# First-stage weights rounded during attention and kept in DRAM, with the first group's sums parked in DRAM

## The chip, the cores and the metric

The kernel runs on one core of a Trainium2 chip. The metric is the device time of one execution in microseconds (us), the median of several runs. Engines are named as the profile names them: PE (matmul), PEld (its weight load), DVE (VectorE), ACT (ScalarE), POOL (GpSimd) and SP, whose queue issues every DMA here.

## The reference

Three stages follow each other. The first is linear attention over 4 batches of 8 heads, 576 tokens, 64 columns a head; the second an MLP of 2048 hidden columns with a leaky slope per column; the third four dense experts of 1024 hidden columns, weighted by the normalised probabilities.

```
proj = x @ w_phi                               # 64 -> 128, for q and for k
proj = proj - max(abs(proj), axis=-1)
phi  = concat(exp(proj), exp(-proj))           # 256 features
kv, z = k_phi.T @ v, sum(k_phi)
attn = (q_phi @ kv) / (q_phi @ z + 1e-6)
h = attn @ w_in;  g = max(h, 0) + alpha * min(h, 0);  y = g @ w_out        # w_in, w_out come as float64
out = sum_e p[e] * (max(y @ w1[e], 0) @ w2[e])
```

Attention output and `y` are 2304 x 512. The weights of the second stage are float64 in DRAM; the kernel rounds them to float32 itself, with integer operations on the two 32-bit words of each number.

## The kernel before

Every large product runs as three fp32r matmuls: a value is split into a high and a low part, and high x high, high x low and low x high are added in PSUM. The hidden columns of both MLP stages are cut in 48 chunks of 128 (16 of the second stage, then 32 of the experts), four to a group, and the 2304 tokens in blocks of 512, 512, 512, 512 and 256. An up block is 12 matmuls of 512 columns (`up_products`, L208), then the activation (`t`, `gh`, `gl`); a down block is 12 matmuls too (`down_chunk`, L234). The sums of a token block over the groups stay in SBUF, in `acc_a` for the first three blocks and in `acc_b` for the other two.

Attention is worked in 16 pairs of heads. For each pair, keys and queries are projected (L348 to L350, three units of 512, 512 and 256 columns each), DVE takes the largest absolute value (`m`, L355) and subtracts it (`pmk`, `pmq`, L362), ACT takes the exponentials of the keys (`ke`, L368), PE forms `kv` (L379, L385), turns it and the queries, and multiplies them (L437); DVE inverts the denominator (`dt`, `di`, `den`, L449 to L452), POOL multiplies and splits. The order of all this is written by a planner (`Plan.run`): it keeps a time for each engine from estimated costs, and takes at each step the operation that can begin first, by rank where several can. The order is then fixed on each engine, which works in it and waits where something is late. The first weight group is rounded and split in the plan too (operations `W`), and the first group's up and down products for token blocks 0 to 2 are filled in between attention's (`U`, `G0` to `G2`, `M`, `C`).

Rounding one weight tile (128 x 512 numbers) takes a 512 KB read, one ACT scaling (L538 in the plan, L176 after it), four DVE instructions (`words`, L168 to L171), one addition, on DVE or POOL (L542, L178), and the split (two more). In the plan, the staging areas are the unused slots 1 and 2 of `acc_a`, which is why the planner's `C` (the copy of a group's sum into `acc_a`) waits for those areas. The other 24 tiles of the second stage are rounded after the plan by `ahead`/`fetch`/`rounded`, two to five steps before their use, in the main loop.

Of the kernel before, what the change touches and what calls it, by code (L numbers as in the profile page):

```python
# [130 lines left out]
def fused(ctx: ExitStack, tc: tile.TileContext, qT, kT, v_main, v_tail, w_phi, alpha, probs, w64, wcat, out):  # L131
# [22 lines left out]
    acc = [acc_a[:, i] for i in range(NA)]  # L154

    def split(src, hi, lo, hi_eng, lo_eng):
        if hi_eng is nc.scalar:
            nc.scalar.copy(hi, src)  # L158
        else:
            hi_eng.tensor_copy(hi, src)  # L160
        lo_eng.tensor_tensor(lo, src, f32(hi), ALU.subtract)  # L161
# [10 lines left out]

    def rounded(w, r, u):

        lo, hi = w[:, 0::2], w[:, 1::2]
        nc.scalar.mul(f32(r), f32(hi), 2.0**-112)  # L176
        words(r, u, lo, hi)
        nc.vector.tensor_tensor(f32(r), f32(r), f32(u), ALU.add)  # L178

    def fetch(c, half, w, st, u):  # L180

        if c < NF1:
            nc.sync.dma_start(st, w64[c, half])
            rounded(st, w.bitcast(U32), u)
        else:
            nc.sync.dma_start(w, wcat[c - NF1, half])
        raw[c, half] = w
# [90 lines left out]
    with ExitStack() as st1:  # L278
# [8 lines left out]
        for args in (  # L287
            ("kr", 1, F32, P, S), ("qr", 1, F32, P, S), ("v", 1, F32, P, len(TILES), 2, D),
            ("kh", 1, F32R, P, S), ("kl", 1, F32R, P, S), ("qh", 1, F32R, P, S), ("ql", 1, F32R, P, S),
            ("m", 13, F32, P, 4), ("pmk", 2, F32, P, 4, F), ("pmq", 3, F32, P, 4, F), ("ke", 2, F32, P, 4, 2, F),  # L290
            ("kvs", 1, F32, P, 4, F), ("qe", 4, F32, P, 2, HMAX), ("kvt", 4, F32, P, 4, P),
            ("den", 2, F32, P, S), ("dt", 1, F32, P, S), ("num", 2, F32, P, S), ("di", 3, F32, P, S // 32, 1),
            ("gh", 5, F32R, P, BLK), ("gl", 5, F32R, P, BLK), ("t", 2, F32, P, BLK),
        ):
            ring(*args)
# [226 lines left out]


        areas = []
        for i in range(2):
            a = acc[1 + i].bitcast(U32)
            areas.append([a[:, :2 * DM], a[:, 2 * DM:3 * DM], a[:, 3 * DM:4 * DM]])
        plan.bufs["area"] = 2
        early = [(0, 0), (1, 0), (0, 1), (1, 1), (2, 0), (3, 0), (2, 1), (3, 1)]

        def w_step(i, k, e):
            c, half = early[i]
            st64, w, u = areas[i % 2]
            lo, hi = st64[:, 0::2], st64[:, 1::2]
# [16 lines left out]
        for i, (c, half) in enumerate(early):  # L551
            costs = ({"d": 1500}, {"a": act(DM)}, {"v": 2 * dve2(DM) + 2 * dve(DM) + 330}, lo_cost(DM), hi_cost(DM), lo_cost(DM))
            for k, cost in enumerate(costs):
                op(("W", k, c, half), cost, [("W", k - 1, c, half)] * (k > 0), RANK["W"] + WSTEP * i,
                   alloc=[("area", i)] * (k == 0), reads=[("area", i)] * (k == 5), late=2000 * (k == 0),
                   emit=lambda e, i=i, k=k: w_step(i, k, e))
# [16 lines left out]
        for blk in range(NA):  # L573
            tok = sum(BLOCKS[blk])
            have = [("X2", p) for p, (b, j) in enumerate(pairs) if b * S < tok]
            for cs in (tuple(range(GRP)),):
# [12 lines left out]
                for i in range(CC):  # L589
# [43 lines left out]
    def ahead(c, half):  # L633
        w = rpool.tile([P, DM], F32, name="w")
        st = u = None
        if c < NF1:
            st = spool.tile([P, 2 * DM], U32, name="st")
            u = upool.tile([P, DM], U32, name="u")
        fetch(c, half, w, st, u)

# [65 lines left out]
```

## Time and profile before

| | us |
|---|---|
| median of 3 runs (1437.93 to 1438.18) | 1438.12 |
| profiled execution, its own time | 1439.93 |
| its span | 1438.2 |
| PE busy / DVE / ACT / POOL | 1418.9 / 654.7 / 412.4 / 212.4 |

The span is what the profile's times count from and to; the profiled execution took 1.7 us more than it. Busy times are summed over the span, so a share says nothing of one stage. Attention with the first blocks fills about the first 300 us, the second stage goes on to about 630 us, the experts fill the rest.

### The profile page before, as it was taken

How to read it: one execution, taken by the hardware profiler on the slowest of the kernel's cores; microseconds unless marked ns; L12 is line 12 of the kernel's file. 1: busy time of each engine (PE TensorE's matmuls, PEld its weight loads, DVE VectorE, ACT ScalarE, POOL GpSimd, SP SyncE). 2: the span in 40 equal slices, each digit the busy share in tenths (PEclk: the TensorE clock that was granted, in tenths of full speed). 3: DMA queues.
4: the chain of work that ended last, by engine and by line, in shares of the span. 5: the costliest groups of instructions: out<-in, count | busy, mean ns of one | idle time of the engine just before them, and what ended most of it. 6: DMA issues, size and time to landing. Idle time of an engine off the chain costs nothing.

```text
span 1438.2 us, 17632 instructions
## 1 busy us (share of the span) xinstructions
PE 1418.9 (99%) x7200; PEld 1152.1 (80%) x7200; DVE 654.7 (46%) x1067; ACT 412.4 (29%) x857; POOL 212.4 (15%) x165
## 2 busy tenths in 40 slices
PE   7999999999999999999999999999999999999998
PEld 4667667778888888888888888888888888888887
DVE  7966656687958855663222222222222222222222
ACT  6877666632212112232021120121210201211110
POOL 3443223102002002011020020020100200200100
PEclk9999999999999999999999999999999999999999
DMA  4311111130202001001020020010100200100001
GB/s 148 112 50 51 50 50 51 53 103 30 88 1 59 30 8 52 1 23 37 0 59 0 1 59 0 8 52 1 30 30 0 59 0 8 52 0 0 30 30 74
DMA packets 25136, 53.67 MB, mean 37 GB/s; under 512 B 3168, under 2 KB 4320, under 8 KB 25056
## 3 DMA queue, kind: packets, MB, share of 16 engines
q1 hardware_dynamic: 25056, 52.55, 12.2%
q8 instruction: 57, 0.93, 0.3%
q14 instruction: 23, 0.19, 0.0%
HBM read 47.82 MB, written 4.72 MB: 37 GB/s over the span
## 4 chain that ended last, share of the span: by engine, by line
PE 94%; DVE 3%; ACT 1%; DMA 1%; issue 0%; SPq 0%; POOL 0%; ACTq 0%; DVEq 0%; POOLq 0%
PE up L208 39%; PE dn L234 39%; PE bank L437 4%; PE kv L379 3%; PE mm L208 2%; PE kv L385 2%; PE mm L234 2%; PE bank L420 1%; PE bank L348 1%; PE bank L349 1%; PE bank L350 1%; DMA st<-w 1%; DMA acc_a<-w 0%; PE bank L401 0%; DVE m L355 0%
## 5 line engine op out<-in xcount | busy, mean ns | idle before, releaser
L208 PE MATMUL up<-Xl,whu 128*128 128x512 f32 (+1 forms) x912 | 334.6, 367 | 0.0
L208 PE MATMUL up<-Xh,whu 128*128 128x512 f32 (+1 forms) x912 | 334.5, 367 | 0.0
L208 PE MATMUL up<-Xh,wlu 128*128 128x512 f32 (+1 forms) x912 | 334.4, 367 | 0.0
L219 ACT ACTIVATE gh<-up 128x512 fp32r<-128x512 f32 (+1 forms) x160 | 88.7, 555 | 539.5 <-PE up L208 539.4
L220 DVE SCALAR_TENSOR_TENSOR gl<-up,gh 128x512 fp32r<-128x512 f32 (+1 forms) x160 | 102.0, 638 | 303.8 <-ACT gh L219 303.7
L234 PE MATMUL dn<-whd,gh 128*128 128x512 f32 x576 | 224.2, 389 | 0.0
L234 PE MATMUL dn<-wld,gh 128*128 128x512 f32 x576 | 224.2, 389 | 0.0
L234 PE MATMUL dn<-whd,gl 128*128 128x512 f32 x576 | 224.1, 389 | 0.0
L208 PEld LDWEIGHTS up<-Xh,whu 128*128 128x128 f32 x912 | 172.0, 189 | 28.6
L208 PEld LDWEIGHTS up<-Xl,whu 128*128 128x128 f32 x912 | 172.0, 189 | 28.4
L208 PEld LDWEIGHTS up<-Xh,wlu 128*128 128x128 f32 x912 | 171.9, 189 | 28.2
L161 POOL TENSOR_TENSOR wlu<-w,whu 128x512 fp32r<-128x512 f32 x44 | 58.2, 1322 | 915.3 <-ACT whu L158 879.7
L234 PEld LDWEIGHTS dn<-whd,gl 128*128 128x128 f32 x576 | 108.1, 188 | 22.5
L234 PEld LDWEIGHTS dn<-whd,gh 128*128 128x128 f32 x576 | 108.2, 188 | 22.1
L234 PEld LDWEIGHTS dn<-wld,gh 128*128 128x128 f32 x576 | 108.2, 188 | 22.1
L271 DVE SCALAR_TENSOR_TENSOR acc_a<-dn,pr,acc_a 128x512 f32<-128x512 f32 x72 | 50.2, 751 | 135.4 <-PE dn L234 135.4
L234 PE MATMUL dn<-gh,wld 128*128 128x512 f32 (+1 forms) x272 | 99.1, 364 | 0.0
L234 PE MATMUL dn<-gh,whd 128*128 128x512 f32 (+1 forms) x272 | 99.1, 364 | 0.0
L234 PE MATMUL dn<-gl,whd 128*128 128x512 f32 (+1 forms) x272 | 99.0, 364 | 0.0
L158 ACT CAST gh<-t 128x512 fp32r<-128x512 f32 (+1 forms) x68 | 38.6, 569 | 134.8 <-DVE t L224 134.6
L437 PE MATMUL bank<-qe,kvt 128*128 128x256 f32 (+1 forms) x256 | 72.6, 417 | 0.9 <-DVE pmk L362 0.9
L158 ACT CAST whu<-w 128x512 fp32r<-128x512 f32 x44 | 27.3, 620 | 136.4 <-PE up L208 121.4
(121 smaller groups left out, 1734.8 us busy)
## 6 DMA issues: line engine op xcount, KB each, us to landing
w<-wcat SPq DMA_DIRECT2D x64, 256.0 KB, 2.6
st<-w SPq DMA_DIRECT2D x24, 512.0 KB, 3.5
kr<-kT SPq DMA_DIRECT2D x16, 288.0 KB, 2.8
qr<-qT SPq DMA_DIRECT2D x16, 288.0 KB, 2.8
out<-o SPq DMA_DIRECT2D x18, 256.0 KB, 2.0
v<-v_main SPq DMA_DIRECT2D x16, 256.0 KB, 3.0
acc_a<-w SPq DMA_DIRECT2D x8, 512.0 KB, 4.5
v<-v_tail SPq DMA_DIRECT2D x16, 32.0 KB, 2.9
```

What stands on the lines that cost most here:

```text
L158: nc.scalar.copy(hi, src)
L161: lo_eng.tensor_tensor(lo, src, f32(hi), ALU.subtract)
L208: nc.tensor.matmul(ps[:, :bn], a[:, cs], x[:, cc, t0:t0 + bn], start=n == 0, stop=n == 3 * CC - 1)
L219: nc.scalar.activation(gh, ps, AF.Relu)
L220: nc.vector.scalar_tensor_tensor(gl, ps, 0.0, f32(gh), ALU.max, ALU.subtract)
L234: nc.tensor.matmul(ps, a, b, start=start and k == 0, stop=stop and k == 2)
L271: nc.vector.scalar_tensor_tensor(av, ps, pe, av, ALU.mult, ALU.add)
L348: nc.tensor.matmul(o, xh[:, tok], wbh, start=True, stop=False)
L349: nc.tensor.matmul(o, xh[:, tok], wbl, start=False, stop=False)
L379: nc.tensor.matmul(kv[h * D:(h + 1) * D, 0], v[:rows, tile_, h], e[:rows, 2 * i + h], start=tile_ == 0, stop=tile_ == len(TILES) - 1, skip ...
L385: nc.tensor.matmul(kv[r:r + 32, 1], ones[:rows], e[:rows, 2 * i + h], start=False, stop=tile_ + 2 >= len(TILES), tile_position=(0, r), ski ...
L437: nc.tensor.matmul(nd[:, :n], tl["kvt", p][:, 2 * h + s], tl["qe", (p, h, c)][:, s, :n], start=s == 0, stop=s == 1)
```

## The change

All 32 tiles of the second stage's weights are now rounded in the plan. The 24 tiles of groups 1 to 3 are not split there: after the addition they are written to DRAM (`wr`, 256 KB each), and the main loop's `fetch` reads them back as float32, as it reads the experts' weights. All three slots of `acc_a` serve as staging areas until the plan ends. The first group's sums can therefore no longer be kept there: they are copied to a new small tile `co`, written to DRAM (`sums`) and read back into `acc_a` when the plan is through. To make room, `kvt` goes from 4 buffers to 3 and `t` from 2 to 1.

```diff
+    sums = [dram.tile([P, CC * BLK], F32, name=f"sums{i}") for i in range(NA)]
+    wr = {(c, half): dram.tile([P, DM], F32, name=f"wr{c}_{half}") for c in range(GRP, NF1) for half in range(2)}
...
-    def fetch(c, half, w, st, u):
-
-        if c < NF1:
-            nc.sync.dma_start(st, w64[c, half])
-            rounded(st, w.bitcast(U32), u)
-        else:
-            nc.sync.dma_start(w, wcat[c - NF1, half])
+    def fetch(c, half, w):
+
+        nc.sync.dma_start(w, wr[c, half] if c < NF1 else wcat[c - NF1, half])
...
-            ... ("qe", 4, F32, P, 2, HMAX), ("kvt", 4, F32, P, 4, P),
+            ... ("qe", 4, F32, P, 2, HMAX), ("kvt", 3, F32, P, 4, P),
-            ("gh", 5, F32R, P, BLK), ("gl", 5, F32R, P, BLK), ("t", 2, F32, P, BLK),
+            ("gh", 5, F32R, P, BLK), ("gl", 5, F32R, P, BLK), ("t", 1, F32, P, BLK), ("co", 2, F32, P, BLK),
...
-        plan.bufs["area"] = 2
+        plan.bufs["area"] = NA
         early = [(0, 0), (1, 0), (0, 1), (1, 1), (2, 0), (3, 0), (2, 1), (3, 1)]
+        early += [(c + i, half) for c in range(GRP, NF1, GRP) for half in range(2) for i in range(GRP)]
...
+            elif c >= GRP:
+                nc.sync.dma_start(wr[c, half], f32(w))
...
-                    op(("C", *key), copy_cost(BLK), [("M", *key)] + [("W", 5, *x) for x in early[:blk + 6] if blk], ...
-                       ... cp(engines[e], acc[a[1]][:, a[2] * BLK:(a[2] + 1) * BLK], tl["mm", a]))
+                    op(("C", *key), copy_cost(BLK), [("M", *key)], pr_ + RANK["G"] - RANK["U"], alloc=[("co", key)],
+                       reads=[("mm", key)], emit=lambda e, a=key: cp(engines[e], new("co", a), tl["mm", a]))
+                    op(("CD", *key), {"d": 1000}, [("C", *key)], ..., reads=[("co", key)], late=2000,
+                       emit=lambda e, a=key: nc.sync.dma_start(sums[a[1]][:, a[2] * BLK:(a[2] + 1) * BLK], tl["co", a]))
...
             plan.run()
+            for i in range(NA):
+                nc.sync.dma_start(acc[i], sums[i])
```

The order moves most on DVE in attention. Before, DVE comes to the first key unit of the thirteenth pair (pair 12) with nothing but attention behind it; these are the last rows up to that unit's subtraction.

```order
L362 TENSOR_TENSOR pmq<-bank,m 64x256
L325 TENSOR_TENSOR ql<-qr,qh 128x576
L355 TENSOR_REDUCE m<-bank 64x2
L362 TENSOR_TENSOR pmk<-bank,m 64x256
L136 COPY num<-bank 64x320
L449 STREAM_TRANSPOSE dt<-den 128x576
L450 TENSOR_SCALAR di<-dt 128x18
L451 RECIPROCAL di<-di 128x18
L452 STREAM_TRANSPOSE den<-di 128x576
L355 TENSOR_REDUCE m<-bank 128x4 x2
L362 TENSOR_TENSOR pmk<-bank,m 128x512 x2
```

In the changed kernel the same place reads so (L173 to L176 are the four `words` instructions, L349 and L356 the maximum and the subtraction).

```order
L173 TENSOR_SCALAR acc_a<-acc_a 128x512
L174 SCALAR_TENSOR_TENSOR acc_a<-acc_a 128x512
L175 TENSOR_SCALAR acc_a<-acc_a 128x512
L176 SCALAR_TENSOR_TENSOR acc_a<-acc_a 128x512
L564 TENSOR_SCALAR t<-mm,alpha_sb 128x512
L565 SCALAR_TENSOR_TENSOR t<-mm,t 128x512
L173 TENSOR_SCALAR acc_a<-acc_a 128x512
L174 SCALAR_TENSOR_TENSOR acc_a<-acc_a 128x512
L175 TENSOR_SCALAR acc_a<-acc_a 128x512
L176 SCALAR_TENSOR_TENSOR acc_a<-acc_a 128x512
L349 TENSOR_REDUCE m<-bank 128x4 x2
L356 TENSOR_TENSOR pmk<-bank,m 128x512 x2
```

Up to this last row DVE has 31 of the 32 rounding steps behind it now, and had 8 there before; 13 of the first group's 24 blocks stand ahead of it on PE, and 8 did before.

At the end of attention, the first matmul of the main loop (`up`) stood before two more up blocks of the plan (`mm`) on PE:

```order
L208 MATMUL mm<-Xh,wlu 128x512
L208 MATMUL up<-Xh,whu 128x512
L208 MATMUL mm<-Xh,whu 128x512
L208 MATMUL mm<-Xl,whu 128x512
L208 MATMUL mm<-Xh,wlu 128x512
```

In the changed kernel the main loop's first matmuls stand between the down matmuls of the plan's last chunk (L202 is the up product, L228 the down product):

```order
L228 MATMUL mm<-gl,whd 128x512
L202 MATMUL up<-Xh,whu 128x512
L202 MATMUL up<-Xl,whu 128x512
L202 MATMUL up<-Xh,wlu 128x512
L202 MATMUL up<-Xh,whu 128x512
L202 MATMUL up<-Xl,whu 128x512
L202 MATMUL up<-Xh,wlu 128x512
L228 MATMUL mm<-gh,whd 128x512
L228 MATMUL mm<-gh,wld 128x512
L202 MATMUL up<-Xh,whu 128x512
L228 MATMUL mm<-gl,whd 128x512
```

Twelve blocks of the first group (four down, four up, four down) came after attention's last product on PE before; seven (three up, four down) come after it now.

On SP's queue, which carried only loads of `kr`, `qr` and `v` in this stage once the eight early reads were through, writes that wait for their data now stand ahead of loads:

```order
L540 DMA wr_1_96<-acc_a 128x512
L540 DMA wr_1_98<-acc_a 128x512
L532 DMA acc_a<-w 128x1024
L599 DMA sums_80<-co 128x512
L540 DMA wr_0_99<-acc_a 128x512
L532 DMA acc_a<-w 128x1024 x2
L331 DMA kr<-kT 128x576
L331 DMA qr<-qT 128x576
```

Each read of a weight tile (L532) waits until the write out of its area has landed, and the next pair's loads wait behind both.

## Rows read from the trace of the kernel before

**Rows 1.** The page's first part: busy time, share of the span, instructions.
```profile
PE 1418.9 (99%) x7200; PEld 1152.1 (80%) x7200; DVE 654.7 (46%) x1067; ACT 412.4 (29%) x857; POOL 212.4 (15%) x165
```

**Rows 2.** Busy time by stretch: length, each engine (instructions), clock, DMA share, GB/s.
```profile
0.00:35.00 35.00, 26.28 (x175) 17.01 (x175) 25.62 (x44) 22.19 (x50) 12.68 (x18) 0.95 0.46 142
35.00:70.00 35.00, 32.70 (x221) 21.74 (x221) 33.89 (x54) 29.29 (x72) 17.73 (x13) 1.00 0.39 124
105.00:280.00 175.00, 175.00 (x1152) 123.19 (x1151) 103.06 (x192) 119.35 (x293) 51.01 (x37) 1.00 0.17 49
280.00:315.00 35.00, 32.34 (x138) 25.46 (x137) 33.40 (x59) 15.70 (x29) 4.56 (x3) 1.00 0.31 91
```

**Rows 3.** DVE's groups by form, 0 to 300 us: busy us, mean ns, idle before.
```profile
L355 DVE TENSOR_REDUCE m<-bank 128x4 f32<-128x512 f32 x64 | 41.5, 674 | 2.5 <-PE bank L350 2.3
...
L362 DVE TENSOR_TENSOR pmk<-bank,m 128x512 f32<-128x512 f32 x32 | 20.6, 675 | 0.0
L355 DVE TENSOR_REDUCE m<-bank 64x2 f32<-64x256 f32 x32 | 13.1, 409 | 8.6 <-PE bank L350 8.6
L452 DVE STREAM_TRANSPOSE den<-di 128x576 f32<-128x576 f32 x16 | 12.4, 778 | 0.6
L449 DVE STREAM_TRANSPOSE dt<-den 128x576 f32<-128x576 f32 x16 | 12.4, 777 | 41.2 <-ACT den L136 41.2
L170 DVE TENSOR_SCALAR acc_a<-acc_a 128x512 uint32<-128x512 uint32 x8 | 8.5, 1065 | 0.6
...
L564 DVE TENSOR_SCALAR t<-mm,alpha_sb 128x512 f32<-128x512 f32 x9 | 6.7, 747 | 6.8 <-PE mm L208 6.8
...
L171 DVE SCALAR_TENSOR_TENSOR acc_a<-acc_a 128x512 f32<-128x512 uint32 x8 | 6.5, 812 | 0.3
L565 DVE SCALAR_TENSOR_TENSOR t<-mm,t 128x512 f32<-128x512 f32 x9 | 6.2, 691 | 0.3
L169 DVE SCALAR_TENSOR_TENSOR acc_a<-acc_a 128x512 uint32<-128x512 uint32 x8 | 5.5, 692 | 0.3
L168 DVE TENSOR_SCALAR acc_a<-acc_a 128x512 uint32<-128x512 uint32 x8 | 4.4, 547 | 2.2 <-ACT acc_a L538 2.2
L451 DVE RECIPROCAL di<-di 128x18 f32<-128x18 f32 x16 | 4.3, 267 | 0.5
...
L450 DVE TENSOR_SCALAR di<-dt 128x18 f32<-128x18 f32 x16 | 3.4, 213 | 0.5
```

**Rows 4.** Timeline, DVE and POOL: start, us, engine, line, operation, operands.
```profile
44.27 0.40 DVE L168 TENSOR_SCALAR acc_a<-acc_a 128x512 uint32<-128x512 uint32 x1
44.70 0.69 DVE L169 SCALAR_TENSOR_TENSOR acc_a<-acc_a 128x512 uint32<-128x512 uint32 x1
...
45.02 1.66 POOL L325 TENSOR_TENSOR ql<-qr,qh 128x576 fp32r<-128x576 f32 x1 [2.03 <-ACT qh L136]
...
45.50 1.46 DVE L170 TENSOR_SCALAR acc_a<-acc_a 128x512 uint32<-128x512 uint32 x1
```

**Rows 5.** Timeline at a key unit of pairs 4 and 12: ACT, DVE, PE.
```profile
76.11 1.15 ACT L368 ACTIVATE ke<-pmk 128x512 f32<-128x512 f32 x2
...
77.58 0.41 DVE L362 TENSOR_TENSOR pmk<-bank,m 64x256 f32<-64x256 f32 x1
...
212.63 1.08 PE L379 MATMUL kv<-ke,v 128*64 128x256 f32 x8
```

**Rows 6.** Timeline of PE after attention: two neighbours, and the two waits.
```profile
293.10 0.39 PE L234 MATMUL mm<-gl,whd 128*128 128x512 f32 x1
293.33 0.39 PE L208 MATMUL mm<-Xh,whu 128*128 128x512 f32 x1
...
300.70 0.50 PE L208 MATMUL mm<-Xh,whu 128*128 128x512 f32 x1 [1.72 <-DVE t L565]
...
304.89 0.50 PE L208 MATMUL mm<-Xh,whu 128*128 128x512 f32 x1 [0.94 <-DVE t L565]
```

**Rows 7.** The page's sixth part: DMA issues, KB each, median us to landing.
```profile
acc_a<-w SPq DMA_DIRECT2D x8, 512.0 KB, 4.5
```

More of the change, by code (lines that the diff above doesn't have):

```diff
@@ L136, in cp @@
         (eng.copy if eng is nc.scalar else eng.tensor_copy)(o, i)
+    dram = pool("dram", 1, space=bass.MemoryType.DRAM)
     const = pool("const", 1)
@@ L171, in words @@
         nc.vector.scalar_tensor_tensor(f32(u), lo, 2.0**-52, f32(u), ALU.mult, ALU.mult)
[L173 to L178, printed above, removed]
-    def fetch(c, half, w, st, u):
-        if c < NF1:
-            nc.sync.dma_start(st, w64[c, half])
-            rounded(st, w.bitcast(U32), u)
-        else:
-            nc.sync.dma_start(w, wcat[c - NF1, half])
+    def fetch(c, half, w):
+        nc.sync.dma_start(w, wr[c, half] if c < NF1 else wcat[c - NF1, half])
         raw[c, half] = w
@@ L290, in fused @@
             ("m", 13, F32, P, 4), ("pmk", 2, F32, P, 4, F), ("pmq", 3, F32, P, 4, F), ("ke", 2, F32, P, 4, 2, F),
-            ("kvs", 1, F32, P, 4, F), ("qe", 4, F32, P, 2, HMAX), ("kvt", 4, F32, P, 4, P),
+            ("kvs", 1, F32, P, 4, F), ("qe", 4, F32, P, 2, HMAX), ("kvt", 3, F32, P, 4, P),
             ("den", 2, F32, P, S), ("dt", 1, F32, P, S), ("num", 2, F32, P, S), ("di", 3, F32, P, S // 32, 1),
-            ("gh", 5, F32R, P, BLK), ("gl", 5, F32R, P, BLK), ("t", 2, F32, P, BLK),
+            ("gh", 5, F32R, P, BLK), ("gl", 5, F32R, P, BLK), ("t", 1, F32, P, BLK), ("co", 2, F32, P, BLK),
         ):
@@ L524, in fused @@
         areas = []
-        for i in range(2):
-            a = acc[1 + i].bitcast(U32)
+        for i in range(NA):
+            a = acc[i].bitcast(U32)
             areas.append([a[:, :2 * DM], a[:, 2 * DM:3 * DM], a[:, 3 * DM:4 * DM]])
-        plan.bufs["area"] = 2
+        plan.bufs["area"] = NA
         early = [(0, 0), (1, 0), (0, 1), (1, 1), (2, 0), (3, 0), (2, 1), (3, 1)]
+        early += [(c + i, half) for c in range(GRP, NF1, GRP) for half in range(2) for i in range(GRP)]
         def w_step(i, k, e):
             c, half = early[i]
-            st64, w, u = areas[i % 2]
+            st64, w, u = areas[i % NA]
             lo, hi = st64[:, 0::2], st64[:, 1::2]
@@ L551, in fused @@
         for i, (c, half) in enumerate(early):
-            costs = ({"d": 1500}, {"a": act(DM)}, {"v": 2 * dve2(DM) + 2 * dve(DM) + 330}, lo_cost(DM), hi_cost(DM), lo_cost(DM))
+            costs = [{"d": 1500}, {"a": act(DM)}, {"v": 2 * dve2(DM) + 2 * dve(DM) + 330}, lo_cost(DM)]
+            costs += [hi_cost(DM), lo_cost(DM)] if c < GRP else [{"d": 1000}]
+            end = len(costs) - 1
             for k, cost in enumerate(costs):
                 op(("W", k, c, half), cost, [("W", k - 1, c, half)] * (k > 0), RANK["W"] + WSTEP * i,
-                   alloc=[("area", i)] * (k == 0), reads=[("area", i)] * (k == 5), late=2000 * (k == 0),
+                   alloc=[("area", i)] * (k == 0), reads=[("area", i)] * (k == end), late=2000 * (k == 0 or end == k == 4),
                    emit=lambda e, i=i, k=k: w_step(i, k, e))
@@ L595, in fused @@
                        emit=lambda e, a=key: down_products(a[0], a[1], a[2], new("mm", a)))
-                    op(("C", *key), copy_cost(BLK), [("M", *key)] + [("W", 5, *x) for x in early[:blk + 6] if blk], pr_ + RANK["G"] - RANK["U"],
-                       reads=[("mm", key)], emit=lambda e, a=key: cp(engines[e], acc[a[1]][:, a[2] * BLK:(a[2] + 1) * BLK], tl["mm", a]))
+                    op(("C", *key), copy_cost(BLK), [("M", *key)], pr_ + RANK["G"] - RANK["U"], alloc=[("co", key)],
+                       reads=[("mm", key)], emit=lambda e, a=key: cp(engines[e], new("co", a), tl["mm", a]))
+                    op(("CD", *key), {"d": 1000}, [("C", *key)], pr_ + RANK["G"] - RANK["U"], reads=[("co", key)], late=2000,
+                       emit=lambda e, a=key: nc.sync.dma_start(sums[a[1]][:, a[2] * BLK:(a[2] + 1) * BLK], tl["co", a]))
         with tc.manual_schedule():
@@ L612, in fused @@
             plan.run()
+            for i in range(NA):
+                nc.sync.dma_start(acc[i], sums[i])
             nc.sync.dma_start(pr, probs)
@@ L621, in fused @@
     wb = [pool("wu2", 2), pool("wd2", 1)]
-    spool = pool("stage", 2)
     rpool = pool("raw", 5)
-    upool = pool("u", 1)
     opool = pool("o", 3)
@@ L634, in ahead @@
         w = rpool.tile([P, DM], F32, name="w")
[L635 to L639, printed above, removed]
+        fetch(c, half, w)
     steps = [(grp, blk) for grp in range(NG) for blk in range(NB)][NA:]
```

## The prediction

> **What bounds the kernel now.** I read the page's first part: PE is busy 99% of the span [rows 1], so nothing done beside PE pays, and time can only be won or lost where PE waits. The stretches show where that is [rows 2]: between 105 and 280 us PE is busy all the time; it is short of full only in the first 70 us (26.28 of 35, then 32.70 of 35) and around the end of attention (32.34 of 35). In the second stretch DVE is busy 33.89 of 35 us: there DVE sets the pace, and it carries the eight early rounding steps. From 105 to 280 us DVE is busy 103.06 of 175 us. At the end of attention DVE is full again (33.40 of 35), with weights being rounded, and PE waits for it twice, 1.72 and 0.94 us [rows 6]. The granted clock is 1.00, the 2.4 GHz level, in all of these but the first stretch (0.95) [rows 2].
>
> So before, the 24 late rounding steps cost PE at most these two waits, 2.7 us together. That is all the change can win there; what it can lose is in attention.
>
> **What goes.** The late rounding leaves DVE, and those two waits were for DVE's `t`. In the changed order three up blocks follow attention. A block takes 12 matmuls of 0.233 us, 2.80 us (293.10 to 293.33) [rows 6]. Counting from the end of attention's last product, DVE first has the last pair's division (2.04 us, from about 0.9 us on) and then the three activations, each 1.44 us for `t` [rows 3] and, taken like one of its two instructions, 0.7 each for `gh` and `gl`, one after the other since `t` has one buffer: `gl` is there at 5.7, 9.3 and 12.1 us. PE is through with the up blocks at 8.4, with nine down matmuls at 10.5, with six of the main loop's at 11.9. It wants the last `gl` at about 12.6. No wait is left, so I book -2.7 us. The reading back of `sums` and `wr` I cost at nothing: the first sum added to `acc_a` comes after two token blocks, some 45 us of PE, and one 512 KB read landed in 4.5 us [rows 7].
>
> **What comes: DVE in attention.** I add up DVE's work to a fixed point, the first key unit of pair 12, where 31 of the 32 rounding steps are behind it. The order gives the counts, rows 3 the durations: 50 maxima of 512 columns at 0.674 (33.7 us) and 24 of 256 at 0.409 (9.8); 49 subtractions at 0.675 (33.1) and 24 at 0.41 (9.8); 10 divisions at 0.777 + 0.213 + 0.267 + 0.778 = 2.04 (20.4); 8 activations at 0.747 + 0.691 (11.5); twelve splits and adds of like size at 0.75 (9.0) and a small one (0.4); and 31 rounding steps at 0.547 + 0.692 + 1.065 + 0.812 = 3.116 us (96.6). The sum is 224.3 us.
>
> How far is such a sum from the clock? In the kernel before, the same count to the third key unit of pair 4, with 8 rounding steps, gives 20 and 10 maxima (13.5 + 4.1), 20 and 9 subtractions (13.5 + 3.7), 3 divisions (6.1), 8 steps (24.9), seven splits and adds (5.3), a small one (0.4): 71.5. That subtraction ended at 77.58 + 0.41 = 77.99 [rows 5]: 6.5 us more, start included. DVE was without a gap to speak of there [rows 2], so I carry the 6.5 over: 230.8 us. The two exponentials of a full unit took 1.15 us for the pair [rows 5] and start about 0.2 after DVE, so the keys' product can begin at 232.2.
>
> When would PE be there by itself? Before, it began this product at 212.63 [rows 5], with 8 blocks of the first group behind it. Now there are 13, five times 2.80 = 14.0 more, and three fewer small matmuls (-0.4): 226.2. PE is therefore 6.0 us late at this point. After it DVE has one rounding step left and falls behind no further, while PE has the same work to do as before; the 6.0 us stay. The lateness is not made in one place: from pair 4 on DVE and PE run nearly even, and DVE loses a little more in each pair.
>
> **The price of one step** decides this, and its ends lie apart. Undisturbed, the four instructions take 0.40, 0.69, 0.40 and 0.69 us (two forms, each twice) [rows 4]: 2.18. In rows 3 the first and third average 0.547 and 1.065. Rows 4 show why: the third was issued at 45.50 while POOL ran from 45.02 for 1.66 us, and took 1.46 us instead of 0.40. So a step pays about 1.06 us where it meets a POOL instruction, and the eight together paid 8 x (3.116 - 2.18) = 7.5 us, about seven meetings. Lower bound 2.18 a step; upper bound two meetings, 4.3. I take 3.116, since POOL was busy 30.4 of 70 us when those eight ran [rows 2] and the changed kernel gives it 29 of the 32 additions beside attention's splits.
>
> The Trainium skill, SBUF — State Buffer, "Who interferes with whom", says DVE and GpSimd share one port pair that is locked for a whole instruction, and that a DVE instruction in a two-port mode, or with two SBUF inputs against a GpSimd one that reads SBUF, waits for it. The trace agrees for the `tensor_scalar` form (1.46 for 0.40 us). By that rule each of a step's four instructions can meet POOL, which makes the dear end a rival below.
>
> **Other things that come.** The planner's order makes DVE wait where it did not: with one buffer of `t`, an activation waits for POOL's `gl` of the chunk before, and a rounding step for its read, which waits for the write out of the area. Nothing in the trace shows these; bounds are 0 and 4% of the 225 us, 9 us (DVE missed 1.1 of 35 us, 3%, in its full stretch [rows 2]). I put 1.0, near the lower end, because DVE runs late against its inputs throughout. ACT gets 24 scalings, 17 us if each takes the 0.7 us of a DVE instruction of that size, in a stretch where it was busy 119.35 of 175 [rows 2]: room for it, no charge. The copies of the sums only change their target.
>
> **Sum.** +6.0 + 1.0 - 2.7 = +4.3 us. The profiled execution took 1439.93 us, 1.7 around its span of 1438.2, so it would come to 1444.2; it lies 1.8 above the median, and against the median of 1438.12 the time is 1442.4 us.
>
> **Rivals.**
> *Rounding is cheap there (faster).* If the steps seldom meet POOL, DVE has room: 105 to 280 us show 72 us of idle time [rows 2], and 24 undisturbed steps need 52. Then PE loses nothing more than in the first 70 us, and the two waits go: 1438.1 - 2.7 = 1435.4. Against it stand seven meetings in eight. The point from which it decides: each of the 23 steps that come on top before pair 12 would have to cost under 3.116 - 4.3/23 = 2.93 us for no loss, and under 3.116 - 7.0/23 = 2.81 for the full gain.
> *Every step meets POOL twice.* 1.06 us more for 31 steps, 8 of them maybe as before: 24 to 33 us on DVE, which PE then waits for: about 1468. POOL's share of 43% speaks against it.
> *The areas turn round too slowly.* A read (4.5 us [rows 7]), scaling (0.7), four instructions (3.1), an addition on POOL (at most the 1.7 of rows 4), and a write, which no row shows and which I estimate at half to all of a read's time, make 12 to 14.5 us; three areas give a step each 4 to 4.8 us, while DVE comes to one each 7.4. But the order has steps in twos and threes, and SP holds the next pair's loads behind a write that waits. If each of some 12 such bunches costs 1 us, the time is 1442.4 + 11 = 1453.
> *It does not save the waits at the end*, because DVE is still late there: then -2.7 falls away, 1445.
>
> **Chances and range.** What a measurement can tell from no change is 0.2%, 2.9 us: under 1435.2 is faster, over 1441.0 slower. My forecast with its neighbour, waits at the end included (1439 to 1448), has 0.54; cheap rounding (under 1439) 0.25, of which 0.09 lies under 1435.2; slow areas (1448 to 1456) 0.14; double meetings 0.07. Of the forecast's own chance 0.12 lies under 1441.0. Faster 0.09, same 0.28, slower 0.63. The range that leaves out two in ten goes from 1436.0 to 1452.0.
>
> **What would show it.** Right: between about 60 and 235 us the profile has DVE busy over 95% and PE short of full by some 7 us in all, waiting for `pmk`, `pmq` and `ke`; the key product of pair 12 begins near 232; L175 averages about 1.0 us; after attention there is no PE wait of over 0.3 us; and from there on PE's pace is unchanged. Wrong: DVE with idle time of 10 us or more between pairs 4 and 11, either because the steps cost 2.2 to 2.8 us (then faster) or because they wait for reads or for POOL (then slower than I say); ACT waiting for a read in front of an exponential; or SP's loads of `kr` and `qr` landing after ACT wants them.

## The result, and the profile after

| | before | after |
|---|---|---|
| median, us (lowest to highest) | 1438.14 (1437.93 to 1438.18) | 1446.09 (1445.24 to 1446.89) |
| span of the profiled execution | 1438.2 | 1443.5 |

The ratio is 1.0055, 95% interval 1.0038 to 1.0073: slower by 7.95 us, in the range (1436.0 to 1452.0), on the side forecast, and 3.7 us above the time forecast. The profiled execution is the fastest of the four, 1445.24 us. The page's first part, against [rows 1]:

```profile
PE 1420.4 (98%) x7200; PEld 1151.8 (80%) x7200; DVE 657.9 (46%) x1036; ACT 412.4 (29%) x862; POOL 246.7 (17%) x191
```

PE has the same 7200 matmuls, DVE the same work (31 rows fewer), POOL 34 us more. The stretches, against [rows 2] (length, each engine with its instructions, clock, DMA share, GB/s; the second and the last two are new cuts):

```profile
0.00:35.00 35.00, 26.42 (x186) 17.73 (x187) 27.63 (x46) 24.30 (x56) 13.39 (x19) 1.00 0.55 173
70.00:105.00 35.00, 30.02 (x190) 19.53 (x190) 32.33 (x54) 23.99 (x57) 17.91 (x13) 0.95 0.45 139
105.00:280.00 175.00, 172.34 (x1102) 121.56 (x1102) 153.45 (x251) 124.98 (x299) 71.26 (x51) 1.00 0.44 138
60.00:235.00 175.00, 167.11 (x1056) 116.79 (x1052) 167.09 (x261) 124.15 (x295) 84.12 (x61) 0.99 0.50 156
75.00:80.00 5.00, 3.84 (x12) 2.62 (x14) 4.97 (x10) 2.77 (x6) 3.49 (x3) 0.66 0.73 256
```

From 105 to 280 us DVE is busy 153 us where it was 103, and PE misses 2.7 us where it missed none. But most is missing before that: 5.0 us of PE between 70 and 105 us, and there the granted clock is 0.95. The kernel before missed 1.8 us there, at a clock of 1.00:

```profile
70.00:105.00 35.00, 33.18 (x225) 22.87 (x224) 22.28 (x42) 25.85 (x63) 14.53 (x11) 1.00 0.18 52
```

The row from 75 to 80 us of the changed kernel finds the low clock: PE ran at the lower level, 1.2 GHz, for part of these 5 us. PE's waits from 30 to 330 us name what it waited for (total, times, longest):

```profile
PE bank L431 <- DVE pmk L356: 4.9, 2, 4.1
PE kv L373 <- ACT ke L362: 3.2, 5, 1.2
...
PE mm L228 <- DVE t L565: 0.4, 1, 0.4
```

One wait of 4.1 us stands out. The timeline of DVE before it (start, us, engine, line, operation):

```profile
64.09 1.50 DVE L173 TENSOR_SCALAR acc_a<-acc_a 128x512 uint32<-128x512 uint32 x1
...
66.35 1.38 DVE L175 TENSOR_SCALAR acc_a<-acc_a 128x512 uint32<-128x512 uint32 x1
...
68.83 1.65 DVE L174 SCALAR_TENSOR_TENSOR acc_a<-acc_a 128x512 uint32<-128x512 uint32 x1
...
71.66 0.77 DVE L443 STREAM_TRANSPOSE dt<-den 128x576 f32<-128x576 f32 x1
...
75.34 1.27 DVE L356 TENSOR_TENSOR pmk<-bank,m 128x512 f32<-128x512 f32 x2
```

POOL's instruction behind the last long one of these (in brackets the idle time before it):

```profile
68.54 1.39 POOL L538 TENSOR_TENSOR acc_a<-acc_a 128x512 f32<-128x512 f32 x1 [1.09 <-DVE acc_a L176]
```

And PE's timeline: the product that waits, the same product 44 us later, and the one late matmul after attention [rows 6]:

```profile
76.16 3.48 PE L431 MATMUL bank<-qe,kvt 128*128 128x256 f32 x8 [4.13 <-DVE pmk L356]
...
120.09 1.99 PE L431 MATMUL bank<-qe,kvt 128*128 128x256 f32 x8
...
312.59 0.47 PE L228 MATMUL mm<-gh,whd 128*128 128x512 f32 x1 [0.42 <-DVE t L565]
```

Two rounding steps stand back to back on DVE (64.09 to 71.74), three of their eight instructions (two in the first step, one in the second) take about 1 us longer than they need, then comes a division, and only then the maxima and the subtraction that empties a PSUM bank. PE wants that bank for its attention product and stands still for 4.13 us; when it goes on, the eight matmuls take 3.48 us instead of 1.99. L174 at 68.83 answers to the third instruction in [rows 4]: it began while POOL ran.

A measure used below: the **lateness** of PE at a pair is the time at which the pair's last attention product begins, less PE's work up to there at its undisturbed pace (0.134 to 0.49 us a matmul by kind, 2.79 a block), worked out from the trace and PE's order. It grows where PE waits or runs slowly, and the order of the work doesn't change it. It can be checked: take the lateness, the waits after attention and half of the time that PE ran at the low clock after attention off the span, and 1417.7 to 1418.4 us are left in every row of this table.

| profiled run | rounding steps in the plan | lateness after pair 2 / pair 4 / the last | waits after attention | span |
|---|---|---|---|---|
| before | 8 | 14.9 / 17.0 / 17.3 | 2.7 | 1438.2 |
| after | 32 | 13.7 / 21.7 / 25.0 | 0.4 | 1443.5 |
| after, run again | 32 | 15.5 / 24.8 / 28.3 | 0.4 | 1446.8 |
| `words` left out | 32, of which 24 without `words` | 14.1 / 18.2 / 18.5 | 0.4 | 1437.0 |
| additions left out | 32, of which 24 without addition | 13.9 / 21.3 / 21.9 | 0.4 | 1440.4 |
| parking only | 8 | 14.2 / 16.2 / 16.2 | 2.2 | 1436.8 |
| one group more | 16 | 14.5 / 23.4 / 23.3 | none | 1441.3 |
| two steps a pair | 32 | 12.3 / 20.1 / 21.1 | 0.4 | 1439.6 |
| before, paced | 8 | 12.1 / 14.6 / 15.2 | 2.2 | 1437.0 |
| three steps to two pairs | 24 | 12.3 / 16.6 / 18.3 | 6.4 | 1444.3 |
| sixteen, paced | 16 | 12.9 / 16.1 / 22.5 | none | 1440.3 |
| twenty-four, paced | 24 | 12.6 / 15.8 / 22.1 | none | 1440.0 |
| one a pair | 16 | 12.7 / 15.9 / 17.5 | 3.0 | 1440.2 |
| booked at 3.2 us | 32 | 31.8 / 39.7 / 42.0 | none | 1459.7 |

For before and after: lateness +7.7, waits after attention 2.2 less, span +5.3. The 17.3 of the kernel before holds up to 1.7 us of a low clock near 12 us, behind a wait of 2.35 us, at the start of its profiled execution:

```profile
10.00:18.00 8.00, 4.81 (x28) 2.42 (x30) 6.00 (x12) 4.86 (x10) 3.25 (x3) 0.79 0.39 134
```

That execution took 1.8 us more than the median of its kernel, and the profiled one of the changed kernel 0.9 us less than its own; this is why the medians lie 7.95 us apart and the two spans only 5.3. The low clock is of the size of the 1.8 us, but no profile of a median execution shows that it is their reason.

### The profile page after: what moved, and what is told of

The parts are those of the page before. It is cut to its first block, busy times and chain, and to the rows that moved or that the text cites. A ratio compares the mean times of both kernels' runs of the same rounds, so it can differ in the third digit from the quotient of the medians.

```text
span 1443.5 us, 17816 instructions
## 1 busy us (share of the span) xinstructions
PE 1420.4 (98%) x7200; PEld 1151.8 (80%) x7200; DVE 657.9 (46%) x1036; ACT 412.4 (29%) x862; POOL 246.7 (17%) x191
## 3 DMA queue, kind: packets, MB, share of 16 engines
q1 hardware_dynamic: 34128, 71.43, 15.9%
## 4 chain that ended last, share of the span: by engine, by line
PE 87%; DVE 9%; issue 2%; ACT 1%; DMA 1%; SPq 0%; POOL 0%; DVEq 0%; ACTq 0%; POOLq 0%
PE up L202 39%; PE dn L228 39%; PE bank L431 2%; PE mm L228 2%; DVE acc_a L174 2%; PE kv L373 2%; DVE m L349 1%; DVE acc_a L173 1%; DVE acc_a L175 1%; PE kv L379 1%; PE bank L414 1%; PE bank L342 1%; DMA acc_a<-w 1%; DVE pmk L356 1%; PE bank L343 1%
## 5 line engine op out<-in xcount | busy, mean ns | idle before, releaser
L202 PE MATMUL up<-Xl,whu 128*128 128x512 f32 (+1 forms) x912 | 334.6, 367 | 0.0
L202 PE MATMUL up<-Xh,whu 128*128 128x512 f32 (+1 forms) x912 | 334.5, 367 | 0.0
L202 PE MATMUL up<-Xh,wlu 128*128 128x512 f32 (+1 forms) x912 | 334.4, 367 | 0.0
L228 PE MATMUL dn<-whd,gh 128*128 128x512 f32 x576 | 224.2, 389 | 0.0
L228 PE MATMUL dn<-wld,gh 128*128 128x512 f32 x576 | 224.2, 389 | 0.0
L228 PE MATMUL dn<-whd,gl 128*128 128x512 f32 x576 | 224.1, 389 | 0.0
L202 PEld LDWEIGHTS up<-Xh,whu 128*128 128x128 f32 x912 | 172.0, 189 | 28.6
L202 PEld LDWEIGHTS up<-Xl,whu 128*128 128x128 f32 x912 | 172.0, 189 | 28.5
L202 PEld LDWEIGHTS up<-Xh,wlu 128*128 128x128 f32 x912 | 171.9, 189 | 28.1
L228 PEld LDWEIGHTS dn<-whd,gl 128*128 128x128 f32 x576 | 108.1, 188 | 22.5
L228 PEld LDWEIGHTS dn<-whd,gh 128*128 128x128 f32 x576 | 108.2, 188 | 22.3
L228 PEld LDWEIGHTS dn<-wld,gh 128*128 128x128 f32 x576 | 108.2, 188 | 22.1
L228 PE MATMUL dn<-gh,wld 128*128 128x512 f32 (+1 forms) x272 | 99.1, 364 | 0.0
L228 PE MATMUL dn<-gh,whd 128*128 128x512 f32 (+1 forms) x272 | 99.1, 364 | 0.0
L228 PE MATMUL dn<-gl,whd 128*128 128x512 f32 (+1 forms) x272 | 99.0, 364 | 0.0
```

What stands on the lines that cost most here:

```text
L202: nc.tensor.matmul(ps[:, :bn], a[:, cs], x[:, cc, t0:t0 + bn], start=n == 0, stop=n == 3 * CC - 1)
L228: nc.tensor.matmul(ps, a, b, start=start and k == 0, stop=stop and k == 2)
```

## The experiments

**Which part costs?** Four kernels. First the 24 added steps without DVE's word instructions:

```diff
             elif k == 2:
-                words(w, u, lo, hi)
+                if c < GRP:
+                    words(w, u, lo, hi)
```

> The changed kernel with the four DVE word instructions of the 24 added rounding steps left out (their weights are then wrong); reads, scaling, addition, write to DRAM, parking of the sums and the order of all the rest stay. Theory 'DVE work in attention': PE's lateness after attention falls from 25.0 us to about 16 to 17 (the kernel before: 17.3), the end waits stay away, time 1434 to 1436. Rival 'traffic and buffers' (writes and reads of the areas, parked sums, one buffer of t and three of kvt): the lateness stays above 22 us, time 1443 to 1446.

1439.95 us (1438.45 to 1441.41), ratio 1.0005 [0.9996, 1.0015]. Everything else of the change is in this kernel, reads, writes, scalings and additions, and the loss can no longer be told from nothing; the lateness is 18.5. Its stretches from 70 to 105 and from 105 to 280 us:

```profile
70.00:105.00 35.00, 31.89 (x209) 21.49 (x209) 20.62 (x37) 27.76 (x68) 19.54 (x15) 1.00 0.56 171
105.00:280.00 175.00, 175.00 (x1129) 124.35 (x1129) 102.26 (x184) 126.16 (x298) 71.04 (x52) 1.00 0.41 132
```

PE is busy all 175 us again, with DVE at 102.26, POOL at 71 and the DMA traffic (132 GB/s) much as in the changed kernel.

Still, the theory's 1434 to 1436 us is missed by 4, although the waits after attention are down to 0.4 us here too. Some 2 us of the loss stay without the added `words`: the lateness grows by 4.1 between pairs 2 and 4, by 2.0 with parking only (below), and the product that waits 4.13 us in the changed kernel still waits half as long, with no low clock behind it:

```profile
74.51 1.97 PE L431 MATMUL bank<-qe,kvt 128*128 128x256 f32 x8 [2.12 <-DVE pmk L356]
```

A division stands ahead of the maxima there, as in the changed kernel; with parking only it stands behind the subtractions. No run tests that order by itself.

The same with the addition left out instead of `words`, so that POOL has less to do:

```diff
             elif k == 3:
-                engines[e].tensor_tensor(f32(w), f32(w), f32(u), ALU.add)
+                if c < GRP:
+                    engines[e].tensor_tensor(f32(w), f32(w), f32(u), ALU.add)
```

> The changed kernel with the final addition of the 24 added rounding steps left out (21 of these run on POOL; the weights are then wrong). DVE keeps all its word instructions. Theory 'DVE work, made dear by meetings with POOL': a step's four instructions fall from 3.2 us to 2.6 to 2.8, the lateness from 25 to 15 to 19 us, time 1435 to 1440. Rival 'DVE work alone, POOL plays no part': a step stays at 3.2 us and the time at 1444 to 1446.

1442.42 us (1442.0 to 1444.02), ratio 1.0025 [1.0016, 1.0034]: nearly half of the loss remains, and the time lies between the theory and its rival. DVE's `words` instructions of the changed kernel by form (busy us, mean ns, idle before), against [rows 3]:

```profile
L174 DVE SCALAR_TENSOR_TENSOR acc_a<-acc_a 128x512 uint32<-128x512 uint32 x32 | 34.8, 1089 | 1.1
...
L175 DVE TENSOR_SCALAR acc_a<-acc_a 128x512 uint32<-128x512 uint32 x32 | 23.3, 728 | 2.8 <-DVE acc_a L174 0.5
L176 DVE SCALAR_TENSOR_TENSOR acc_a<-acc_a 128x512 f32<-128x512 uint32 x32 | 23.2, 727 | 1.1
L173 DVE TENSOR_SCALAR acc_a<-acc_a 128x512 uint32<-128x512 uint32 x32 | 21.4, 670 | 3.5 <-ACT acc_a L534 3.5
```

Without the additions, the first of them:

```profile
L174 DVE SCALAR_TENSOR_TENSOR acc_a<-acc_a 128x512 uint32<-128x512 uint32 x32 | 26.2, 820 | 1.1
```

A step costs 1.089 + 0.728 + 0.727 + 0.670 = 3.21 us in the changed kernel and 0.820 + 0.703 + 0.756 + 0.640 = 2.92 without the additions, 9.4 us over the 32; three additions that ran on DVE, 2.1 us, are gone too. Yet the lateness falls only by 3.1, not into the theory's 15 to 19, since the 4.1 us wait and the low clock at 76 us are still there.

Parking of the sums, three areas and the smaller buffers alone, with groups 1 to 3 rounded in the main loop as before:

```diff
-        early += [(c + i, half) for c in range(GRP, NF1, GRP) ...]
+        early += [(c + i, half) for c in range(GRP, LIM, GRP) ...]      # LIM = 4: none
```

> Parking alone: first group's sums through DRAM, three areas, t with one buffer, kvt with three, but only the eight early rounding steps in attention; the other 24 in the main loop as before. Theory 'DVE work in attention': lateness 15.5 to 17.5 us as before, DVE waits at the end of attention still there, time 1436.5 to 1438.5. Rival 'parking and buffers cost': 1440 to 1445.

1438.76 us (1438.11 to 1440.84), ratio 1.0000 [0.9991, 1.0009]. Parking costs nothing and brings nothing that can be told from nothing, as the theory had it; its 1436.5 to 1438.5 was just missed.

With `LIM = 8` one group is added, so 16 steps in the plan:

> Eight of the 24 late steps (group 1) are rounded in attention and kept in DRAM, the other 16 in the main loop as before. Theory 'what counts is how crowded DVE is while steps are taken as early as possible': the eight come at once after the first eight, lateness about 20 to 21 us (between 17.3 and 25), end waits gone or smaller, time 1438.5 to 1441. Rival 'cost in proportion to steps': a third of the whole, 1440 to 1441. Rival 'DVE has 70 us of idle time later, so eight steps are free': 1435 to 1436.5.

1442.38 us (1441.41 to 1444.49), ratio 1.0023 [1.0013, 1.0032]. A third of the added steps, and nearly half of the loss, more than the theory and the rivals gave it; the profiled run has 6.0 of the changed kernel's 7.7 us of lateness, all of it by pair 4. The wait is the same, and the low clock behind it lasted longer, as PE's timeline and the stretch behind the wait show:

```profile
77.02 3.75 PE L443 MATMUL bank<-qe,kvt 128*128 128x256 f32 x8 [4.14 <-DVE pmk L368]
```

```profile
75.00:85.00 10.00, 7.98 (x44) 4.51 (x44) 7.65 (x15) 5.88 (x14) 5.62 (x5) 0.66 0.51 166
```

So the cost does not go by the number of steps, and the bunch at 64 us is part of it. It is also not a matter of DVE's sum: DVE is busy only 114.46 of the 175 us after 105 us there, and PE does not make up for what it lost.

**Does spreading the steps help?** In three kernels the `words` of step i may only be placed behind a given pair's division.

```diff
+                   behind=[("I", min(14, (i - 1) // 2))] * (k == 2 and (min(14, (i - 1) // 2)) >= 0),
```

> The changed kernel with one thing altered: the word instructions of rounding step i may stand on DVE only behind the division of pair (i-1)//2, so that at most two steps come to a pair; steps, reads, writes and parked sums are the same in number. Theory 'place on DVE': by the sums of DVE's work up to each unit, DVE's lead over PE's need never falls as far as before, lateness about 11 to 13 us (before 17.3, changed kernel 25.0), no waits at the end, time 1429 to 1433. Rival 'the added work, traffic and meetings with POOL cost wherever they stand': lateness above 20, time 1440 to 1446.

1441.55 us (1439.55 to 1442.65), ratio 1.0017 [1.0008, 1.0027]: better than the changed kernel (1447.79 in the same session, below), and still slower than before. The theory's 1429 to 1433 is missed; the time and the lateness (21.1) are those that the rival gave. The first 70 us improve (lateness 12.3 after pair 2), and one event at 89 us, here in PE's timeline, gives it back:

```profile
89.41 3.78 PE L431 MATMUL bank<-qe,kvt 128*128 128x256 f32 x8 [3.04 <-DVE pmk L356]
```

The same pacing in the kernel before (`(i - 1) // 2`, its 8 steps):

> The kernel before, its eight early steps paced in the same way (step i behind the division of pair (i-1)//2), nothing else. Theory 'place on DVE': the lateness falls from 17.3 to 11 to 13 us, the two waits at the end (2.7 us) stay, time 1432 to 1435. Rival 'the first 70 us are bound by other chains (start, exponentials, transposes)': lateness 15 to 17, time 1436 to 1438.5.

1439.01 us (1437.82 to 1440.94), ratio 1.0000 [0.9990, 1.0009]. Lateness falls by 2.1, to the rival's 15 to 17; up to 1.7 of that is the low clock near 12 us, which this profiled run lacks. And in it a wait of 2.25 us for `t` after attention comes with a clock of 0.72 over 6 us. No gain that can be measured.

Two groups more, three steps to two pairs (`LIM = 12`, `(2 * i - 2) // 3`):

> Groups 1 and 2 rounded in attention (24 steps in all, three to two pairs), group 3 in the main loop as before, paced. Theory 'place on DVE': lateness 10.5 to 12.5 us, no waits at the end, time 1428.5 to 1432.5, as low as two per pair or lower. Rival as there: above 1438.

1447.13 us (1444.78 to 1449.92), ratio 1.0057 [1.0040, 1.0074]. A miss: attention is nearly undisturbed, and the loss moved behind it. The last two steps each met POOL in three of their four instructions and took 5.4 and 5.1 us; the second in DVE's timeline is

```profile
303.00 0.41 DVE L174 TENSOR_SCALAR acc_a<-acc_a 128x512 uint32<-128x512 uint32 x1
303.44 1.66 DVE L175 SCALAR_TENSOR_TENSOR acc_a<-acc_a 128x512 uint32<-128x512 uint32 x1
305.14 1.39 DVE L176 TENSOR_SCALAR acc_a<-acc_a 128x512 uint32<-128x512 uint32 x1
306.56 1.63 DVE L177 SCALAR_TENSOR_TENSOR acc_a<-acc_a 128x512 f32<-128x512 uint32 x1
```

and the last activation comes behind them; PE's timeline has the wait for it:

```profile
312.10 0.80 PE L240 MATMUL mm<-gh,whd 128*128 128x512 f32 x1 [6.35 <-DVE t L578]
```

The changed kernel, unaltered, in a later session:

> The changed kernel once more, unaltered, for a second profile. If the spread of its times (1445.2 to 1446.9) comes from where the clock's low stretch falls and how often a step meets POOL, lateness 24.5 to 27 us in this profile and the long wait of PE near 72 us is there again; if the wait near 72 us was an accident of one execution, it is absent and the lateness lower by 4 or more.

1447.79 us (1445.41 to 1448.59), ratio 1.0055 [1.0038, 1.0072], as at first. Its profiled run took 3.3 us more span than that of the table above. The lateness, 28.3, is above the 27 expected. The wait before 78 us is the same to 0.01 us; the clock was low longer behind it, and once more near 12 us, and these two make nearly all of the 3.3 us. Its product in PE's timeline, and the two stretches:

```profile
77.96 3.75 PE L431 MATMUL bank<-qe,kvt 128*128 128x256 f32 x8 [4.12 <-DVE pmk L356]
```

```profile
10.00:20.00 10.00, 6.99 (x48) 3.54 (x47) 8.08 (x16) 6.95 (x16) 4.01 (x4) 0.83 0.48 160
75.00:85.00 10.00, 7.04 (x30) 3.95 (x30) 8.55 (x16) 4.47 (x10) 6.54 (x5) 0.66 0.49 162
```

**With the planner told the measured price.** It books 2.2 us for a step's `words`; these three book 3.2 (`{"v": 3200}`), and two of them pace the steps as well: one a pair for the first eight, then two a pair (16 steps) or three (24).

Sixteen steps:

> Only group 1 is added to the early steps (16 in all, groups 2 and 3 in the main loop as before); one step behind each of the first seven divisions, then two to a pair up to pair 9; the planner books 3200 ns for a step's word instructions. Theory 'DVE's bunches in front of the units PE waits for, and the low clock after a long wait': no wait of PE over 2 us in attention, lateness 12 to 14.5 us, end waits under 1 us, no low clock stretch but a chance one, time 1432 to 1435.5, below both kernels. Rival 'lateness has a floor near 15 to 17 us from other chains': 1436 to 1438.5.

Twenty-four:

> As before it, with groups 1 and 2 early (24 in all), three to a pair from pair 6 to 11, group 3 in the main loop. Theory: DVE has 17 us a pair and needs 9 plus 1.4 plus three steps of 3.2, some 20, so it eats up a lead of about 16 us over six pairs without PE waiting: lateness 12 to 15.5 us, time 1432 to 1436. If a step meets POOL more often than once (4 to 5 us a step, as in the paced run with 24), lateness 18 to 22 and time 1438 to 1443.

All 32, not paced:

> The changed kernel with one number altered: the planner books 3200 ns instead of 2206 for a step's word instructions. Plain thought: an order from a truer price waits less, lateness 15 to 20, time 1436 to 1441. Theory 'sum of DVE's work up to the unit PE wants': in this order 62 word and add instructions stand ahead of pair 4's units (45 in the changed kernel), the sum puts PE late by 7 us more than the changed kernel, lateness 30 to 34, time 1450 to 1455.

Sixteen: 1443.09 us (1442.29 to 1444.06), ratio 1.0033 [1.0021, 1.0046]. Twenty-four: 1443.70 (1441.78 to 1445.59), 1.0038 [1.0025, 1.0052]. Both miss what I expected. Up to pair 7 they are as good as the kernel before (lateness 16.1 and 15.7), then both lose some 6 us at one place: the wait below and the half of 6.8 us of low clock. DVE's timeline of the sixteen-step kernel there:

```profile
148.53 1.32 DVE L174 TENSOR_SCALAR acc_a<-acc_a 128x512 uint32<-128x512 uint32 x1
149.88 1.64 DVE L175 SCALAR_TENSOR_TENSOR acc_a<-acc_a 128x512 uint32<-128x512 uint32 x1
151.55 1.52 DVE L176 TENSOR_SCALAR acc_a<-acc_a 128x512 uint32<-128x512 uint32 x1
153.11 1.67 DVE L177 SCALAR_TENSOR_TENSOR acc_a<-acc_a 128x512 f32<-128x512 uint32 x1
...
157.29 0.38 DVE L368 TENSOR_TENSOR pmk<-bank,m 64x256 f32<-64x256 f32 x1
```

POOL's in the same time:

```profile
147.68 1.88 POOL L331 TENSOR_TENSOR ql<-qr,qh 128x576 fp32r<-128x576 f32 x1 [2.51 <-ACT qh L137]
149.53 1.44 POOL L550 TENSOR_TENSOR acc_a<-acc_a 128x512 f32<-128x512 f32 x1
150.93 1.86 POOL L331 TENSOR_TENSOR kl<-kr,kh 128x576 fp32r<-128x576 f32 x1
152.75 1.47 POOL L558 TENSOR_TENSOR wld<-acc_a,whd 128x512 fp32r<-128x512 f32 x1
```

PE's wait, and the stretch behind it:

```profile
158.53 0.91 PE L385 MATMUL kv<-ke,v 64*64 64x256 f32 x4 [2.56 <-ACT ke L374]
```

```profile
158.00:166.00 8.00, 7.46 (x34) 5.96 (x35) 7.15 (x9) 4.28 (x11) 4.05 (x3) 0.57 0.48 169
```

POOL runs four instructions without a pause, and each of the step's four waits for one of them: 6.2 us where 2.18 are needed. The last key subtraction of the pair stands behind this step and a division, PE waits 2.56 us for the exponential, and the clock is at 0.57 over the next 8 us.

The higher price alone, without pacing: 1463.36 us (1461.69 to 1465.21), ratio 1.0175 [1.0160, 1.0191]. Slower, as the theory had it, though by more than it said. The planner now puts more steps ahead of the first pairs (8 before the first division on DVE, 5 in the changed kernel), PE waits up to 3.1 us several times, and the clock falls again and again between 28 and 56 us, as this stretch shows:

```profile
28.00:56.00 28.00, 21.56 (x113) 14.49 (x109) 26.86 (x38) 18.47 (x42) 17.86 (x13) 0.82 0.39 121
```

**The same steps at other places.** The sixteen-step kernel once more with the last eight steps one behind each division instead of two: up to 148 us DVE's order is the same, then the step that took 6.2 us is behind the next division, and the last step ends only at 297 us.

```diff
-  behind=[("I", i - 1 if i < 8 else 6 + (i - 8) // 2)] * ...
+  behind=[("I", i - 1)] * (k == 2 and i > 0),
```

> The sixteen paced steps once more, but strictly one step behind each pair's division. Up to 148 us DVE has the same instructions in the same order as in the sixteen-step kernel before it; there that step came next which found POOL busy through all four of its instructions and took 6.2 us, and the step now stands behind the next division. Theory (the loss sits at single places where DVE comes late with a subtraction, and a wait of PE of some 2.5 us or more brings the low clock behind it): the wait of 2.6 us at 155.6 us and the 6.8 us of low clock are gone, attention ends with PE some 16 us behind its undisturbed pace instead of 22.5, and the time falls by about 6 us to 1436 to 1438, or to 1434 to 1436 if no late `t` keeps PE waiting at the end. Rival (the loss goes by the number of steps, and the place was chance): the same sixteen steps cost the same, 1442 to 1444, with a wait of that size at another place.

1442.75 us (1441.90 to 1445.77), ratio 1.0031 [1.0019, 1.0043]. Half a hit: the place is the theory's, the time the rival's, and so is a wait of that size elsewhere. The place is cured as expected, with the same number of steps: the subtraction comes 7.8 us earlier, and the lateness ends at 17.5 instead of 22.5. DVE's timeline has it at

```profile
149.51 0.42 DVE L368 TENSOR_TENSOR pmk<-bank,m 64x256 f32<-64x256 f32 x1
```

The time is the same all the same, because now a `t` is late at the end, and the clock falls once more. DVE's timeline there:

```profile
305.55 0.76 DVE L469 TENSOR_TENSOR Xl<-num,Xh 128x576 fp32r<-128x576 f32 x1 [2.03 <-ACT Xh L137]
```

POOL's, ahead of it:

```profile
297.92 1.29 POOL L550 TENSOR_TENSOR acc_a<-acc_a 128x512 f32<-128x512 f32 x1
299.18 2.54 POOL L167 TENSOR_TENSOR wlu<-w,whu 128x512 fp32r<-128x512 f32 x2
301.68 1.28 POOL L167 TENSOR_TENSOR wld<-w,whd 128x512 fp32r<-128x512 f32 x1
302.93 1.88 POOL L465 TENSOR_TENSOR num<-num,den 128x576 f32<-128x576 f32 x1
```

PE's wait, and the stretch behind it:

```profile
307.84 0.47 PE L240 MATMUL mm<-gh,whd 128*128 128x512 f32 x1 [2.96 <-DVE t L578]
```

```profile
308.00:313.00 5.00, 5.00 (x16) 3.93 (x16) 2.83 (x4) 0.96 (x2) 0.00 (x0) 0.66 0.00 0
```

POOL does the addition of the last rounding step (L550) and splits three weight tiles of the main loop before it multiplies the last pair's `num`; DVE waits for what follows from that, with the activation behind it in its order. That this is the cause is read from the trace; no run moved the splits. The addition stands there because the last steps were moved towards the end of attention, so this run does not separate the cure at 148 us from a loss that the move itself may have made.

No version beat the kernel before. The parking alone and the paced kernel before equal it. That the loss sits at single places is shown by the waits and the low clock behind them; no kernel with more than eight steps and its `words` in it confirms it with a time as low as before.

## Why the prediction was right and where it was wrong

**Where the loss comes from: right.** Without the 24 `words` most of it is gone, and parking with its buffers costs nothing that can be told; some 2 us stay with the rest of the change. DVE was busy 167.09 of 175 us from 60 to 235 us (95.5%; over 95% was forecast) and PE short by 7.9 (7 forecast). That the 7 came out is luck in part, since 4.1 of the 7.9 are the one wait. The key product of pair 12, in PE's timeline, began at 233.84, against 232.2 forecast and 212.63 before [rows 5]:

```profile
233.84 1.08 PE L373 MATMUL kv<-ke,v 128*64 128x256 f32 x8 [0.19 <-ACT ke L362]
```

**The mis-sized term is the +6.0.** At that product PE was 233.84 - 226.2 = 7.6 us late, 7.7 at the end of attention and 11.0 in the second profiled run. The step price was 3.21 us instead of 3.116, near enough; 31 steps of it put 3.0 us on the sum, and the sum then gives 233.8 for DVE's subtraction, which ended at 233.1. That it came so near is luck in part. The sum adds durations, and neighbours on DVE overlap: two subtractions of 0.675 us took 1.27 together in the row at 75.34. Between 76 and 233 us such overlaps make 10.6 us that the sum counts twice, and DVE stood still for 7.4 us that it leaves out. Nor is the sum the whole cause: without the additions DVE has over 9 us less to do and the lateness falls by 3.1.

Of the 3.7 us between the median and the forecast only 1.0 lies in the forecast's own sum (+5.3 between the two profiled executions, +4.3 forecast); the rest is how far these two lie from their medians.

**The step that failed is the sentence that the lateness is not made in one place.** Between pairs 2 and 4 the changed kernel lost 8.0 us (13.7 to 21.7) and the kernel before 2.1, so 5.9 more; after pair 4 it lost 3.0 more than the kernel before. Up to pair 2 it was 1.2 better, because of the low clock near 12 us in the profile before; 5.9 + 3.0 - 1.2 make the 7.7. The wait of 4.13 us and the low clock behind it are 5.8 of the 8.0. With `words` left out 4.1 are lost in the same place, so some 2 of the 5.9 are not the rounding's. A sum of DVE to a far point says nothing of a bunch ahead of one subtraction, and I had put no price on what follows a long wait: 3.48 instead of 1.99 us for the first eight matmuls, 1.5 us in this run, more where the low clock lasted longer. In the two profiled executions of the changed kernel, 1445.24 and 1448.59 us, the longer low clock makes nearly all of the difference; that it makes the spread of the other times (1445.4 to 1448.6 in the second set) is likely and not shown.

**The +1.0 for other waits of DVE** can't be told apart: from 76 to 233 us DVE was busy 149.57 of 157, so it missed 7.4 us, of which I can't say which part PE paid for.

**The -2.7: right.** After attention one wait of 0.42 us is left, so 2.2 went. "No wait over 0.3" was slightly too strict: this wait was for the second `t`, and the prediction had followed `gl`. Its times for `gl`, 9.3 and 12.1, also hold about 0.7 us more than the terms that it names (which give 8.6 and 11.5); that is the size of the split `Xl` on DVE, 0.75 us, which stands between them. The pace after it is unchanged: from 700 to 1050 us PE is busy all the time in both kernels, with 1636 matmuls in each.

**Which instruction meets POOL: wrong, without effect on the sum.** I expected L175 at about 1.0 us because the third instruction averaged 1.065 before [rows 3]; it took 0.728, and the second, L174, took 1.089 instead of 0.692. In the changed order POOL's addition for the step before begins just ahead of the second one: at 68.54, and L174 at 68.83 took 1.65 us. The Trainium skill, SBUF — State Buffer, "Who interferes with whom", says that a DVE instruction with two SBUF inputs contends with a GpSimd one that reads SBUF. The traces now agree for that form too (1.65 us instead of 0.69).

**The rivals.** Cheap rounding would have needed steps under 2.93 us; they took 3.21. Slow areas: a read of a tile landed in 4.1 us against 4.5 [rows 7], a write in 2.2, and between 20 and 290 us ACT waited for a read only once, 0.4 us. Steps that met POOL three or four times came singly, at 5.1 to 6.2 us, and in three of the five paced versions of the changed kernel they stand ahead of the longest wait; as an average they did not come.

What stays open: whether an order exists that keeps both attention and its end free. The runs paced the steps and gave the planner their price; they did not tell it of POOL.

## What to carry over

Add up an engine's work to each point where the busy engine needs it, not to one far point: a bunch ahead of one subtraction costs at once, and where the busy engine then stands still for some microseconds, look at the granted clock behind the wait. When a late piece is cured in a fixed order, read the next wait down the line before you count the gain: here every paced version of the changed kernel lost at another place. A price given to a planner helps only with the order it then makes: the truer one cost 17 us.

## What had not been expected of the hardware

The clock. In these traces the granted clock fell to 1.2 GHz during or just behind waits of PE such as those of 2.56, 3.04, 4.13 and 6.35 us above, in the kernel before too (a wait of 2.35 us that ends at 12.34, with 0.79 over the 8 us from 10 on). Not every such wait did it: behind the 2.12 us with `words` left out the clock stayed at 1.00, and behind one of 2.48 us that ends at 16.28 in the one-a-pair kernel too. It was low for 3.4 or 6.8 us at a time, once for 10.2 (the higher price, from 100 us on). At half speed that is up to 1.7 or 3.4 us on top of the wait, and less where the fall comes while PE still waits. With like waits (4.13 and 4.12 us) it lasted 3.4 us in one execution of the changed kernel and 6.8 in the other.

A chain of POOL instructions holds up all four instructions of a step, one after the other: 6.2 us for 2.18 us of work.
